# Attention with clusters, then experts: later turns for the second expert, own gathers first, one more drain

## The chip, the cores and the metric

The kernel runs on one core of one Trainium2 chip. The metric is the device time of one execution in microseconds. The kernel before took 926.72 us (median of three runs, 924.52 to 931.46).

## The reference, cut to what matters

The inputs are q, k and v of 4 batches, 8 heads, 768 positions and 64 dimensions, 16 centroids per head, two gates and the weights of 8 experts. A query sees the keys of its own cluster alone. The result, read as 3072 rows of 512, goes row by row through the one expert that its gate picks:

```python
for e in range(E):                      # E = 8, F = 1024
    mask = e_idx == e
    h = np.maximum(x[mask] @ w1[e], 0.0)
    ye = h @ w2[e]
    out[mask] = gate_w[mask, None] * eom[mask, e, None] * ye
```

The gate picks 400, 354, 531, 257, 408, 444, 274 and 404 rows for experts 0 to 7. How many rows an expert has decides which code runs for it.

## The kernel before, in words

The first 560 us are attention and routing: TensorE makes maxima, scores and values, and at the end every row of x stands in DRAM (`x_d`), with a list per expert of the numbers of its rows (`list_d`, read into `lst`). The rest is the expert stage, which the change is about.

**Sizes.** For every expert the program holds one branch for each of 41 sizes, 256 to 512 rows in steps of 8 and on to 768 in steps of 32. Each engine reads the size and jumps (`tc.Switch`). Up to 512 rows an expert is one chunk. Beyond that (`v >= NONE`, here expert 2 with 531 rows, run as 2 x 272) it is two chunks, and the second chunk's rows, 68 to each of four gathers, are the "own" gathers into `XG[2]` by the indices `lsxi`.

**One chunk.** `chunk` runs f = 0 to 7. In each step TensorE makes a hidden tile (`hidden`, L1145: 12 matmuls into `ps_h`), then projects the step before (`project`, L1164: 12 matmuls into `ps_y`), then does what `beside(f)` asks for. ScalarE and VectorE turn `ps_h` into `hh` and `hl` (L1152, L1153), and split a weight tile four steps ahead into `wh` and `wl` (L1043, L1044) from a staging buffer that SyncE loaded (L1038).

**Turns and gathers.** While expert e runs, GpSimd gathers the rows of expert e + 2 from `x_d` into `XG` (`gather`, L1047, four of 128 rows each), and the rows of expert e + 1, gathered earlier, are turned (`turn`: four transposes into `ps_xg`, L1133, a cast `xh`, L1134, a subtraction `xl`, L1135). In the kernel before, `after(f)` does one turn and one gather at each of f = 2 to 5 (`TF = 2`). For expert 1 the list itself is read only in expert 0 at f = 1 (`first_lists`), and its four gathers follow at once.

**Results.** Behind the chunk ScalarE and VectorE copy `ps_y` into `yt` (L1182). Four transposes per 128 rows, a scaling into `yo` and a scatter to the output (`finish`, L1209) follow: for most experts behind the next expert's chunk, for a large expert's first chunk within its second, for the last expert but one within the last, at f = 0 to 3 (`before`), and for the last one behind it. The program ends with the waits for all transfers, a drain of each engine and a barrier.

**What sets the order.** TensorE's, VectorE's and ScalarE's order within an expert is that of the code, or a scheduler's by priorities; GpSimd's within an expert is the scheduler's. Each engine runs its queue in order. GpSimd issues all gathers and scatters, on one queue.

Of the kernel before, what the change touches and what calls it, by code (L numbers as in the profile page):

```python
# [20 lines left out]
DM, E, FF = 512, 8, 1024  # L21
# [12 lines left out]
NVAR, NONE, XCH = len(SIZES), SIZES.index(512) + 1, 512  # L34
# [5 lines left out]
def tile_cluster_attention_moe(  # L40
# [10 lines left out]
    nc = tc.nc  # L51
# [114 lines left out]
    V, QD, KD, hold = {}, {}, {}, {}  # L166
# [764 lines left out]
    def maxs():  # L931
        for u in range(2, NU):
            yield from maxima(u)
            yield

    gx = maxs()
# [86 lines left out]
    XG, XH, XL = [None] * 3, [None] * 3, [None] * 3  # L1023
# [22 lines left out]
    def gather(xg, idx, t, n=P):  # L1046
        return nc.gpsimd.indirect_dma_start(  # L1047
            xg[0:n, t], None, x_d, bass.IndirectOffsetOnAxis(ap=idx[0:n, t:t + 1], axis=0),
            bounds_check=CAP - 1, oob_is_err=False,
        )  # L1050
# [54 lines left out]
    with tc.issue_after(hold['ctl'].ins), tc.issue_after(hold['act'].ins):  # L1105
# [8 lines left out]
        a, min_val=lo, max_val=hi, skip_runtime_bounds_check_because="counts of tokens bound it"  # L1114
# [6 lines left out]
    def w_ahead(e, f, own, nxt):  # L1121

        for n, fn in ((LL, w_load), (LS, w_split)):
            if f + n < NF:
                if own:
                    fn(e, f + n)
            elif nxt:
                fn(e + 1, f + n - NF)

    def turn(k, t):  # L1130
        ps = p_t.tile([P, NC, P], F32, name="ps_xg", tag="tr")
        for c in range(NC):
            nc.tensor.transpose(ps[:, c], XG[k][:, t, c * P:(c + 1) * P], ident)  # L1133
        nc.scalar.copy(XH[k][:, :, t], ps)  # L1134
        hold['xl', t] = nc.vector.tensor_tensor(XL[k][:, :, t], ps, XH[k][:, :, t].bitcast(F32), ALU.subtract)  # L1135
# [44 lines left out]
    def result(d, py, yt):  # L1180

        (nc.vector.tensor_copy, nc.scalar.copy)[d % 2](yt[:, d].rearrange("p t m -> p (t m)"), py[d])  # L1182

    def chunk(k, n4, py, beside, e=E):

        prev = None
        for f in range(NF):
            h = hidden(f, XH[k], XL[k], n4)
            if prev is not None:
                project(f - 1, prev, py, n4)  # L1190
            beside(f)
            prev = h
        hint(e)
        project(NF - 1, prev, py, n4)

    AE = {ET.Activation}
    TF = 2

    def finish(yt, ls, idx, t, others, eng=None, pool=None, tag="tr"):

        ps = (pool or p_t).tile([P, NC, P], F32, name="ps_yo", tag=tag)
        for d in range(NC):
            nc.tensor.transpose(ps[:, d], yt[:, d, t], ident)
        yo = mp.tile([P, DM], F32, name="yo", tag="yo", bufs=4)
        if eng is nc.vector:
            nc.vector.tensor_scalar(yo, ps.rearrange("p d c -> p (d c)"), ls[:, t, 1:2], None, ALU.mult)
        else:
            nc.scalar.activation(yo, ps.rearrange("p d c -> p (d c)"), AF.Copy, scale=ls[:, t, 1:2])  # L1208
        sc = nc.gpsimd.indirect_dma_start(  # L1209
            out, bass.IndirectOffsetOnAxis(ap=idx[:, t:t + 1], axis=0), yo, None,  # L1210
            bounds_check=CAP - 1, oob_is_err=False,
        )
        for o in others:
            tc.declare_no_dep(sc.ins, o.ins, reason="every token has a row of its own")
        others.append(sc)
# [3 lines left out]
    lsxi = mp.tile([P, 4], I32, name="lsxi")  # L1219

    def expert(e, v):
        n = SIZES[v]
        a, y = e % 2, YT[e % 2]
        others = []
        if e == 0:
            first_turn()

        def before(f):

            if e == E - 1 and f < 4:  # L1230
                finish(YT[1 - a], lst[:, e - 1], rowsi[:, e - 1], f, others)

        def after(f):
            if e + 1 < E and TF <= f < TF + 4:
                turn(1 - a, f - TF)
                if e + 2 < E:
                    gather(XG[a], rowsg[:, e + 2], f - TF)

        if v < NONE:
            def beside(f):  # L1240
                if e == 0 and f == 1:
                    first_lists()
                w_ahead(e, f, True, True)
                before(f)
                after(f)
            chunk(a, n // 4, PY, beside, e + 1)
            return

        n4 = n // 8
        nc.sync.dma_start(  # L1250
            lsx[0:n4], list_d[e * CAP + n // 2:e * CAP + n].rearrange("(p t) x -> p t x", t=4)
        )
        nc.vector.tensor_copy(lsxi[0:n4], lsx[0:n4, :, 0])
        for t in range(4):
            gather(XG[2], lsxi, t, n4)

        def beside1(f):
            if e == 0 and f == 1:
                first_lists()
            w_ahead(e, f, True, False)  # L1260
            before(f)
            if f >= 4:
                turn(2, f - 4)

        def beside2(f):
            w_ahead(e, f, False, True)
            if f < 4:
                finish(y, lst[:, e], rowsi[:, e], f, others)
            after(f)

        chunk(a, n4, PY, beside1)
        for d in range(NC):
            result(d, PY, y)
        chunk(2, n4, PY, beside2, e + 1)

        nc.vector.memset(rowsi[:, e], int(FAR))
        nc.vector.tensor_copy(rowsi[0:n4, e], lsxi[0:n4])
        nc.vector.tensor_copy(lst[0:n4, e], lsx[0:n4])
# [27 lines left out]
    rowsg = mp.tile([P, E, 4], I32, name="rowsg")  # L1306
    behind = mp.tile([1, 2], F32, name="behind")

    def first_turn():

        for t in range(4):
            turn(0, t)
            keep_warm(W3 if t < 3 else W4, ps=PY[t])
            if t % 2:
                with tc.issue_after(hold['xl', t].ins):
                    for f in ((1,), (2, 3))[t // 2]:
                        w_split(0, f)

        bh = nc.sync.dma_start(behind, XG[0][0:1, 3, 0:2])
        with tc.issue_after(bh.ins):  # L1320
            for f in range(NSTG, LL):
                w_load(0, f)

    def first_lists():
        sh = [P, E, 4]
        nc.gpsimd.dma_start(
            lst, list_d[0:E * CAP].rearrange("(e s) x -> e s x", e=E)[:, 0:512].rearrange("e (p t) x -> p e t x", t=4)
        )
        nc.vector.tensor_tensor(
            rows, slot4.rearrange("p (o t) -> p o t", o=1).broadcast_to(sh),  # L1330
            ctl[:, 3].rearrange("p (e o) -> p e o", o=1).broadcast_to(sh), ALU.is_ge,
        )
        nc.vector.tensor_scalar(rows, rows, FAR, None, ALU.mult)

        with tc.issue_after(hold['hl'].ins):
            nc.vector.tensor_scalar(rowsg, lst[:, :, :, 0], CAP - 1.0, None, ALU.min)
        with tc.issue_after(hold['hl'].ins):
            nc.vector.tensor_tensor(rowsi, rows, lst[:, :, :, 0], ALU.add)
        for t in range(4):
            gather(XG[1], rowsg[:, 1], t)  # L1340
        nc.gpsimd.memset(XG[2], 0.0)

    for e in range(E):
        for v in tc.Switch(vvar[e], NVAR, hint=f"expert{e}"):
            with tc.manual_schedule(engines=AE):
                expert(e, v)
        with tc.manual_schedule(engines={ET.PE, ET.Activation, ET.DVE}):
            others = []
            a = e if e == E - 1 else e - 1
            for d in range(NC):  # L1350
                result(d, PY, YT[e % 2])
                if d % 2 and 0 < e < E - 1:
                    for t in (d - 1, d):
                        finish(
                            YT[a % 2], lst[:, a], rowsi[:, a], t, others, (nc.scalar, nc.vector)[t % 2],
                            (p_h, p_t)[d // 2], ("h", "tr")[d // 2],
                        )
            if e == 0:
                keep_warm(W5, p_t, "tr")
            if e == E - 1:  # L1360
                for t in range(4):
                    finish(YT[a % 2], lst[:, a], rowsi[:, a], t, others, (nc.scalar, nc.vector)[t % 2])
# [39 lines left out]
```

## Time and profile before

| what | us |
|---|---|
| median of three runs | 926.72 |
| the profiled execution | 928.52 |
| its span, first to last instruction | 926.8 |
| TensorE busy (matmul) | 830.4 |
| GpSimd busy | 433.7 |
| mean granted clock of TensorE | 0.952 |

The span is cut by the engines' own instructions; the profiled execution's time holds 1.7 us more than the span. A timeline row gives an instruction's start and length, and in brackets how long its engine had stood idle and what ended that. An engine that stands idle costs time only if the end of the program waits for it; in the expert stage that is TensorE, and behind the last matmul it is GpSimd's queue.

### The profile page before, as it was taken

How to read it: one execution, taken by the hardware profiler on the slowest of the kernel's cores; microseconds unless marked ns; L12 is line 12 of the kernel's file. 1: busy time of each engine (PE TensorE's matmuls, PEld its weight loads, DVE VectorE, ACT ScalarE, POOL GpSimd, SP SyncE). 2: the span in 40 equal slices, each digit the busy share in tenths (PEclk: the TensorE clock that was granted, in tenths of full speed). 3: DMA queues.
4: the chain of work that ended last, by engine and by line, in shares of the span. 5: the costliest groups of instructions: out<-in, count | busy, mean ns of one | idle time of the engine just before them, and what ended most of it. 6: DMA issues, size and time to landing. Idle time of an engine off the chain costs nothing.

```text
span 926.8 us, 14485 instructions
## 1 busy us (share of the span) xinstructions
PE 830.4 (90%) x4907; PEld 633.4 (68%) x4907; DVE 501.7 (54%) x1013; ACT 394.1 (43%) x757; POOL 433.7 (47%) x329
## 2 busy tenths in 40 slices
PE   4798969999799998999989989799799799999991
PEld 3445646666566565666656446799799799999991
DVE  5767536567466576556764375445424455446511
ACT  3234445555255553555425543334325344335421
POOL 6634547767677766777575444500501321402201
PEclk9789879999999999999999999899989899999996
DMA  8652864565656555455110055743702644535301
GB/s 233 143 120 59 199 164 128 145 164 133 105 150 162 126 155 121 121 155 128 28 35 35 1 152 128 231 142 113 240 12 70 204 157 157 172 106 181 124 18 40
DMA packets 47387, 117.18 MB, mean 126 GB/s; under 512 B 11460, under 2 KB 13740, under 8 KB 47180
## 3 DMA queue, kind: packets, MB, share of 16 engines
q1 hardware_dynamic: 40300, 99.71, 40.1%
q0 software_dynamic: 6880, 15.28, 5.0%
q8 instruction: 60, 0.98, 0.5%
q14 instruction: 147, 1.20, 0.4%
HBM read 61.48 MB, written 15.95 MB: 84 GB/s over the span
## 4 chain that ended last, share of the span: by engine, by line
PE 43%; issue 21%; DMA 20%; DVE 10%; POOL 2%; SPq 1%; ACT 1%; POOLq 0%; DVEq 0%; ACTq 0%
PE ps_xt L487 14%; PE ps_ex L454 14%; DMA xg<-x_d,rowsg 7%; DMA out_dram<-yo,rowsi 6%; PE ps_mx L414 6%; DVE mx L418 5%; DMA x_d<-xn 3%; DMA xg<-x_d,rows 2%; PE ps_sm L508 2%; PE ps_as L217 2%; POOL out_dram L1209 1%; PE ps_xn L625 1%; DMA m<-qd 1%; PE ps_lg L578 1%; POOL xg L1047 1%
## 5 line engine op out<-in xcount | busy, mean ns | idle before, releaser
L418 DVE TENSOR_REDUCE mx<-ps_mx 128x1 f32<-128x384 f32 x360 | 181.9, 550 | 125.3 <-PE ps_mx L414 123.6
L459 ACT ACTIVATE ex<-ps_ex 128x384 f32<-128x384 f32 x384 | 169.7, 490 | 152.5 <-PE ps_ex L454 122.3
L474 POOL TENSOR_TENSOR es<-es,ex 128x768 f32<-128x768 f32 (+1 forms) x128 | 185.3, 1469 | 88.4 <-ACT ex L459 87.7
L454 PE MATMUL ps_ex<-m,s 128*128 128x384 f32 (+1 forms) x768 | 185.5, 362 | 7.1 <-DMA m<-nmt 7.0
L454 PEld LDWEIGHTS ps_ex<-m,s 128*128 128x128 f32 (+1 forms) x768 | 137.9, 197 | 45.8 <-issue 18.7
L487 PE MATMUL ps_xt<-ex,v 128*64 128x384 f32 (+1 forms) x768 | 148.0, 505 | 0.0
L1209 POOL DMA_INDIRECT out_dram<-yo,rowsi x36 | 37.0, 1027 | 230.0 <-ACT yo L1208 175.6
L414 PE MATMUL ps_mx<-s,m 96*128 96x384 f32 x360 | 110.8, 376 | 13.5 <-DVE xn L646 5.2
L487 PEld LDWEIGHTS ps_xt<-ex,v 128*64 128x64 f32 x768 | 52.4, 139 | 69.4 <-issue 66.2
L414 PEld LDWEIGHTS ps_mx<-s,m 96*128 96x128 f32 x360 | 68.8, 197 | 38.0 <-DVE mx L418 25.4
L1164 PE MATMUL ps_y<-hh,wh 128*128 128x272 f32 (+6 forms) x288 | 92.9, 323 | 0.0
L1044 DVE TENSOR_TENSOR wl<-wst,wh 128x1024 fp32r<-128x1024 f32 x64 | 78.3, 1225 | 26.4 <-ACT wh L1043 25.1
L1164 PE MATMUL ps_y<-hh,wl 128*128 128x272 f32 (+6 forms) x288 | 92.4, 321 | 0.0
L1164 PE MATMUL ps_y<-hl,wh 128*128 128x272 f32 (+6 forms) x288 | 91.9, 322 | 0.0
L1153 DVE SCALAR_TENSOR_TENSOR hl<-ps_h,hh 128x272 fp32r<-128x272 f32 (+6 forms) x72 | 37.3, 517 | 100.8 <-ACT hh L1152 95.0
L1152 ACT ACTIVATE hh<-ps_h 128x272 fp32r<-128x272 f32 (+6 forms) x72 | 33.1, 459 | 123.9 <-PE ps_h L1145 110.3
L1145 PE MATMUL ps_h<-xh,wh 128*128 128x272 f32 (+6 forms) x288 | 63.8, 345 | 8.8 <-issue 7.0
L474 POOL TENSOR_TENSOR es<-ex,ex 128x768 f32<-128x768 f32 (+1 forms) x32 | 54.9, 1730 | 32.9 <-ACT ex L459 32.9
L1043 ACT CAST wh<-wst 128x1024 fp32r<-128x1024 f32 x64 | 66.6, 1043 | 3.8 <-DMA wst<-in_ww_dram 3.8
L1145 PE MATMUL ps_h<-xh,wl 128*128 128x272 f32 (+6 forms) x288 | 59.5, 329 | 0.0
L1145 PE MATMUL ps_h<-xl,wh 128*128 128x272 f32 (+6 forms) x288 | 59.3, 329 | 0.0
L1164 PEld LDWEIGHTS ps_y<-hh,wh 128*128 128x128 f32 x288 | 54.5, 189 | 0.5
(246 smaller groups left out, 1122.5 us busy)
## 6 DMA issues: line engine op xcount, KB each, us to landing
wst<-in_ww_dram SPq DMA_DIRECT2D x64, 512.0 KB
m<-hi SPq DMA_DIRECT2D x64, 192.0 KB
s<-hi SPq DMA_DIRECT2D x64, 192.0 KB
qd<-in_qT_dram SPq DMA_DIRECT2D x16, 384.0 KB
kd<-in_kT_dram SPq DMA_DIRECT2D x16, 384.0 KB
v<-in_vp_dram SPq DMA_DIRECT2D x16, 384.0 KB
m<-qd SPq DMA_DIRECT2D x32, 192.0 KB
s<-kd SPq DMA_DIRECT2D x32, 192.0 KB
```

The source lines that it names most:

```text
L414: nc.tensor.matmul(ps[:, :HF], m1[0:96, h, t * P:(t + 1) * P], s1[0:96, h, f * HF:(f + 1) * HF], start=True, stop=True,)
L418: nc.vector.tensor_reduce(mx2[:, h, t, f:f + 1], ps[:, :HF], AX.X, ALU.max)
L454: nc.tensor.matmul(ps[f][:, :HF], s[0:kk, h, kt * P:(kt + 1) * P], m[0:kk, h, f * HF:(f + 1) * HF], start=j == 0, stop=j == 1,)
L459: nc.scalar.activation(ex[:, cols(f)[0]], ps[f][:, :HF], AF.Exp, scale=0.125)
L474: eng.tensor_tensor(es, a, ex[:, o2], ALU.add)
L487: nc.tensor.matmul(xt[f][h * D:(h + 1) * D, :c.stop - c.start], V[u][:, kt, h * D:(h + 1) * D], ex[h][:, c], start=kt == 0, stop=kt == KT - 1,
L1043: nc.scalar.copy(wh, st)
L1044: nc.vector.tensor_tensor(wl, st, wh.bitcast(F32), ALU.subtract)
L1145: hold['mm'] = nc.tensor.matmul(psv, w[:, c * P:(c + 1) * P], x[:, c, :, 0:n4], start=k == 0, stop=k == 3 * NC - 1,)
L1153: hold['hl'] = nc.vector.scalar_tensor_tensor(hl[:, :n], ps[:, :n], 0.0, hh[:, :n].bitcast(F32), ALU.max, ALU.subtract)
L1164: nc.tensor.matmul(py[d].rearrange("p (t m) -> p t m", t=4)[:, :, 0:n4], w[:, DM + d * P:DM + (d + 1) * P], x, start=f == 0 and k == 0, st ...
L1209: sc = nc.gpsimd.indirect_dma_start(out, bass.IndirectOffsetOnAxis(ap=idx[:, t:t + 1], axis=0), yo, None, bounds_check=CAP - 1, oob_is_err ...
```

## The change

It does three things. In expert 0 the turns of expert 1 (and the gathers of expert 2 that stand with them) are placed at f = 4 to 7; for the other experts nothing moves. In an expert with more than 512 rows the gathers for the next expert but one are ordered behind the last of its own four gathers. In the last expert GpSimd gets one drain, ordered behind the fourth scatter of its loop.

```diff
--- before.py
+++ after.py
@@ -1231,10 +1231,15 @@
                 finish(YT[1 - a], lst[:, e - 1], rowsi[:, e - 1], f, others)
 
         def after(f):
-            if e + 1 < E and TF <= f < TF + 4:
-                turn(1 - a, f - TF)
+            if e == E - 1 and f == 5:
+                with tc.issue_after(others[3].ins):
+                    nc.gpsimd.drain()
+            first = TF if e else 4
+            if e + 1 < E and first <= f < first + 4:
+                turn(1 - a, f - first)
                 if e + 2 < E:
-                    gather(XG[a], rowsg[:, e + 2], f - TF)
+                    with tc.issue_after(hold['gx'].ins) if v >= NONE else nullcontext():
+                        gather(XG[a], rowsg[:, e + 2], f - first)
 
         if v < NONE:
             def beside(f):
@@ -1252,7 +1257,7 @@
         )
         nc.vector.tensor_copy(lsxi[0:n4], lsx[0:n4, :, 0])
         for t in range(4):
-            gather(XG[2], lsxi, t, n4)
+            hold['gx'] = gather(XG[2], lsxi, t, n4)
 
         def beside1(f):
             if e == 0 and f == 1:
```

VectorE at the end of expert 0, in the branch for 400 rows, before (`wl` is half of a split weight tile, `xl` half of a turn, `hl` half of a hidden tile):

```order
L1153 SCALAR_TENSOR_TENSOR hl<-ps_h,hh 128x400
L1044 TENSOR_TENSOR wl_5736<-wst_5724,wh_5728 128x1024
L1135 TENSOR_TENSOR xl_6055<-ps_xg,xh_6054 128x4x128
L1153 SCALAR_TENSOR_TENSOR hl<-ps_h,hh 128x400
L1044 TENSOR_TENSOR wl_5737<-wst_5725,wh_5729 128x1024
L1153 SCALAR_TENSOR_TENSOR hl<-ps_h,hh 128x400
L1178 SWITCH_STRIDE
L1178 ISA
L1178 BRANCH_PREFETCH_HINT
L1044 TENSOR_TENSOR wl_5738<-wst_5726,wh_5730 128x1024
L1398 UNCONDITIONAL_BRANCH
```

And now:

```order
L1044 TENSOR_TENSOR wl_5736<-wst_5724,wh_5728 128x1024
L1135 TENSOR_TENSOR xl_6055<-ps_xg,xh_6054 128x4x128
L1153 SCALAR_TENSOR_TENSOR hl<-ps_h,hh 128x400
L1044 TENSOR_TENSOR wl_5737<-wst_5725,wh_5729 128x1024
L1135 TENSOR_TENSOR xl_6055<-ps_xg,xh_6054 128x4x128
L1153 SCALAR_TENSOR_TENSOR hl<-ps_h,hh 128x400
L1178 SWITCH_STRIDE
L1178 ISA
L1178 BRANCH_PREFETCH_HINT
L1044 TENSOR_TENSOR wl_5738<-wst_5726,wh_5730 128x1024
L1135 TENSOR_TENSOR xl_6055<-ps_xg,xh_6054 128x4x128
L1403 UNCONDITIONAL_BRANCH
```

The last two turns stand in the last two steps, and the last `xl` is VectorE's last instruction before the branch. TensorE's transposes and ScalarE's casts moved with them.

GpSimd in expert 2's branch for 544 rows, before (`xg_6056` is `XG[2]`, `xg_5718` is `XG[0]`, for expert 4):

```order
L1398 UNCONDITIONAL_BRANCH
L1344 BRANCH_PREFETCH_HINT
L1047 DMA xg_5718<-x_d,rowsg 128x512 x4
L1047 DMA xg_6056<-x_d,lsxi 68x512 x4
L1209 DMA out_dram<-yo,rowsi 3072x512 x4
L1398 UNCONDITIONAL_BRANCH
```

And now:

```order
L1403 UNCONDITIONAL_BRANCH
L1349 BRANCH_PREFETCH_HINT
L1047 DMA xg_6056<-x_d,lsxi 68x512 x4
L1047 DMA xg_5718<-x_d,rowsg 128x512 x4
L1209 DMA out_dram<-yo,rowsi 3072x512 x4
L1403 UNCONDITIONAL_BRANCH
```

The two groups of four gathers have changed places. The drain stands in none of these rows; in the last expert's branch it is the instruction right behind the fourth scatter.

## Rows read from the trace of the kernel before

**Rows 1.** The page's busy times (busy us, share of the span, instructions) and the clock that TensorE was granted in 40 equal slices of the span, in tenths.

```profile
PE 830.4 (90%) x4907; PEld 633.4 (68%) x4907; DVE 501.7 (54%) x1013; ACT 394.1 (43%) x757; POOL 433.7 (47%) x329
PEclk9789879999999999999999999899989899999996
```

**Rows 2.** The waits of TensorE from 560 to 727 us: who waited <- what ended the wait: us in total, times, longest. The three longest.

```profile
PE ps_xg L1133 <- DMA xg<-x_d,lsxi: 7.2, 1, 7.2
PE ps_h L1145 <- issue: 6.7, 1, 6.7
PE ps_xg L1133 <- DMA xg<-x_d,rowsg: 4.7, 1, 4.7
```

**Rows 3.** Windows of the expert stage: from:to, us, then busy time (and instructions) of PE, PEld, DVE, ACT and POOL, then the granted clock, the share of the transfer engines and GB/s.

```profile
569.70:582.40 12.70, 12.70 (x69) 11.78 (x69) 7.06 (x11) 6.82 (x9) 3.15 (x3) 1.00 0.86 204
582.54:587.19 4.65, 0.00 (x1) 0.00 (x1) 2.06 (x3) 0.00 (x0) 3.73 (x4) 0.86 0.66 204
587.19:592.70 5.51, 5.51 (x18) 5.48 (x19) 0.69 (x1) 0.94 (x2) 4.29 (x5) 0.50 0.90 305
666.56:673.73 7.17, 0.01 (x2) 0.04 (x1) 0.44 (x1) 0.00 (x0) 2.88 (x3) 0.82 0.74 205
673.73:678.03 4.30, 4.30 (x20) 4.30 (x21) 0.72 (x2) 0.98 (x2) 0.00 (x0) 0.50 0.02 4
912.20:926.80 14.60, 0.00 (x0) 0.00 (x0) 0.00 (x0) 0.00 (x0) 0.01 (x1) 0.50 0.05 18
```

**Rows 4.** Timeline of TensorE: start us, us, engine, line, operation, tiles, shape [idle before <- what ended it]. The first turn of the first expert, two turns of expert 1 (within expert 0), and the first hidden matmuls and the first use of `hl` of expert 1.

```profile
565.32 0.63 PE L1133 MATMUL ps_xg<-ident,xg 128*128 128x128 f32 x4 [1.73 <-DMA xg<-x_d,rows]
587.19 1.12 PE L1133 MATMUL ps_xg<-ident,xg 128*128 128x128 f32 x4 [4.65 <-DMA xg<-x_d,rowsg]
604.33 0.60 PE L1133 MATMUL ps_xg<-ident,xg 128*128 128x128 f32 x4
617.12 1.01 PE L1145 MATMUL ps_h<-xh,wh 128*128 128x360 f32 x4
621.97 0.50 PE L1164 MATMUL ps_y<-hl,wh 128*128 128x360 f32 x2
```

**Rows 5.** Timeline of VectorE at the end of expert 0, with the same columns: the last turn's `xl`, the last `wl`, the copies of the result, and the first `hl` of expert 1.

```profile
605.58 0.69 DVE L1135 TENSOR_TENSOR xl<-ps_xg,xh 128x512 fp32r<-128x512 f32 x1 [0.56 <-ACT xh L1134]
613.05 1.23 DVE L1044 TENSOR_TENSOR wl<-wst,wh 128x1024 fp32r<-128x1024 f32 x1 [0.36 <-ACT wh L1043]
617.44 1.29 DVE L1182 COPY yt<-ps_y 128x512 f32<-128x512 f32 x2 [3.16 <-issue]
620.28 0.53 DVE L1153 SCALAR_TENSOR_TENSOR hl<-ps_h,hh 128x360 fp32r<-128x360 f32 x1 [1.55 <-ACT hh L1152]
```

**Rows 6.** Timeline of GpSimd: the issue of the first gather for expert 0 and of the first for expert 1.

```profile
560.15 1.63 POOL L1047 DMA_INDIRECT xg<-x_d,rows  x1 [7.05 <-DVE ctli L1099]
582.02 1.90 POOL L1047 DMA_INDIRECT xg<-x_d,rowsg  x1 [4.53 <-DVE rowsi L1338]
```

**Rows 7.** Timeline of GpSimd and TensorE at the start of expert 2: the last of the four scatters behind expert 1, the first gather for expert 4, the first own gather, and the first two turns of the own rows.

```profile
656.51 1.68 POOL L1209 DMA_INDIRECT out_dram<-yo,rowsi  x1 [0.30 <-issue]
658.95 1.04 POOL L1047 DMA_INDIRECT xg<-x_d,rowsg  x1 [0.76 <-issue]
664.25 1.45 POOL L1047 DMA_INDIRECT xg<-x_d,lsxi  x1 [0.30 <-issue]
673.73 1.09 PE L1133 MATMUL ps_xg<-ident,xg 128*128 128x128 f32 x4 [7.17 <-DMA xg<-x_d,lsxi]
679.17 0.60 PE L1133 MATMUL ps_xg<-ident,xg 128*128 128x128 f32 x4
```

**Rows 8.** Timeline of GpSimd in the last expert: the fourth scatter in its loop and the next instruction.

```profile
886.31 0.97 POOL L1209 DMA_INDIRECT out_dram<-yo,rowsi  x1 [3.95 <-ACT yo L1208]
907.41 0.97 POOL L1209 DMA_INDIRECT out_dram<-yo,rowsi  x1 [20.12 <-ACT yo L1208]
```

**Rows 9.** The queue instructions by line (engine and operation, count: shortest/median/longest ns, first to last start in us): INC_SWDGE_SEM from 565 to 590 us, the same from 860 to 890 us, the one at the end, the drains at the end, and TensorE's branches.

```profile
L1398 POOLq INC_SWDGE_SEM  x8: 441/476/509, 567.5 to 587.1; - x8
L1398 POOLq INC_SWDGE_SEM  x4: 1187/1202/1222, 873.9 to 881.2; - x4
L1363 POOLq INC_SWDGE_SEM  x1: 2096/2096/2096, 915.4 to 915.4; - x1
L1398 POOLq DRAIN  x3: 46/109/8134, 917.8 to 926.5; - x3
L1398 PEldq COMPARE_BRANCH  x16: 321/570/6287, 561.1 to 902.3; - x16
```

**Rows 10.** The transfers that GpSimd issued, by tiles, with their counts, from the view of the DMA issues.

```profile
out_dram<-yo,rowsi POOLq DMA_INDIRECT x36
xg<-x_d,rowsg POOLq DMA_INDIRECT x28
list_d<-lists,rposi POOLq DMA_INDIRECT x24
xg<-x_d,rows POOLq DMA_INDIRECT x4
xg<-x_d,lsxi POOLq DMA_INDIRECT x4
lst<-list_d POOLq DMA_DIRECT2D x1, 32.0 KB
```

## The prediction

> **What bounds the kernel now.** I read the busy times and the clock line first, then TensorE's waits over the expert stage, then the windows around each wait, the timelines of the engines that end them, and last GpSimd's own queue behind the last scatter. TensorE is busy 90% of the span [rows 1], so the time goes where it stands still, and a stop can be paid twice: once idle, once more at the lower clock afterwards. In the expert stage (from about 560 us) three stops are over 4 us [rows 2]: 4.7 us for a gather with `rowsg`, 7.2 us for a gather with `lsxi`, and 6.7 us before a `ps_h` that no named work ends. The first two are what two parts of the change touch; the third lies at a branch and is left alone. [...] The idle of 1.73 us before the very first expert's rows [rows 4] left the clock at 1.00 [rows 3].
>
> After the last work the span still lasts 14.6 us in which no engine computes [rows 3]. Of it, GpSimd's queue holds one INC_SWDGE_SEM of 2.10 us and one DRAIN of 8.13 us [rows 9].
>
> **Part 1, the turns of expert 1.** The change adds no instruction: four turns (four transposes, a cast, a subtraction each) move from f = 2 to 5 to f = 4 to 7. In the trace the first is reached at 582.54 and its rows come at 587.19, since the gather was issued at 582.02 [rows 4, 6]. In the new order TensorE goes on with the hidden tile of f = 3, and meets the first turn two tiles later; a step without a turn takes (604.33 - 587.19 less the slow stretch's loss of 2.75) / 3 turns, 4.8 us with its turn, so some 4.4 us without, and it comes at about 582.5 + 2 x 4.4 = 591.3, 4 us behind the landing. The 4.65 us go. The half-speed stretch gives back half of 5.51, 2.75 us. The three later turns follow at 4.8 us each; the gathers behind the first are issued 1.3 us apart, so none is late.
>
> What the move costs stands at the other end. The last turn now lies in front of the last projection, and the last instruction of VectorE before the branch becomes `xl` in place of `wl`. A turn's `xl` starts 1.25 us after its transposes [rows 4, 5]: at 613.24 + 1.25 = 614.5 on the old scale, 1.44 us behind the `wl` at 613.05. Behind that instruction VectorE needed 4.4 us until its first copy, 3.16 of them with nothing to wait for that the profile shows, and its `hl` for expert 1 came at 620.28 [rows 5]; both slide by 1.44 us. TensorE first reads that `hl` at 621.97 [rows 4], and it would be ready at 620.28 + 1.44 + 0.53 = 622.25. I charge 0.3 us, with 0 and 1.5 as the ends. Expert 1 itself starts at 617.12 [rows 4], behind 614.5 + 0.7. The gathers for expert 3 that wait for these turns are late by a turn or two, but GpSimd has nothing else to issue before the scatters behind expert 1, so that is free. Weight loads issue on SyncE in the same order; one split moves forward with TensorE, and I cost it at nothing because its staging load was issued before the gathers. If that cover went, a split would hold `hh` and cost as much as the wait it replaces. **Part 1: 4.65 + 2.75 - 0.3 = 7.1 us, between 5.9 and 7.4.**
>
> **Part 2, the large expert's own gathers first.** Expert 2 alone takes this path. GpSimd issues four scatters until 658.2, then the four gathers of expert 4's rows (needed only an expert later), then the own ones from 664.25 on [rows 7]. TensorE stood at its turn from 666.56 and got its rows at 673.73, 9.48 us after that issue. Swapped, the first own gather is issued in the place of the other, 658.95. How long it takes there no row shows. Nearest from below: 5.17 us from issue to TensorE's start, twice, at 560.15 to 565.32 and 582.02 to 587.19 [rows 4, 6], with no transfer of GpSimd's close ahead. From above: the 9.48 us of the same gather with four transfers ahead. In the new place four scatters are ahead, of which the first three have had longer to land, so I take the middle, 7.3: rows at 666.3, just in time, with 664.1 and 668.4 as ends (no wait, or 1.9 us). The other three are issued 1.5 us apart and are needed 3.5 us apart. The four gathers now behind them have until expert 3. So 7.17 us of idle and half of 4.30 us of slow clock go, 9.3 in all. I take **9.0**, leaving 0.3 for a short wait; the lower end, 1.9 us waited and the clock falling all the same, is 9.3 - 1.9 - 2.1 = **5.3**.
>
> [...]
>
> **Part 3, the drain.** DRAIN stands three times at the end: 8134, 109 and 46 ns [rows 9]. The long one runs when all transfers have been waited for, and the next takes 0.1 us, so its length is work that one drain does away with. What work, the INC_SWDGE_SEM rows hint at: the same instruction takes 0.44 to 0.51 us around 580 us and 1.2 us around 880 us [rows 9]; it grows as GpSimd issues transfers. There are 36 + 28 + 24 + 4 + 4 + 1 = 97 of them [rows 10], and 8134 / 97 is 84 ns each. The added drain sits behind the fourth scatter of the last expert, which ends at 887.28, when 93 have been issued: some 7.8 us. GpSimd's next work starts at 907.41, after 20.1 us of idle [rows 8]; nobody waits for GpSimd in between, so it is free up to 20 us. At the end four transfers are left: 4 x 84 ns + 0.1 = 0.45 us in place of 8.13, and about 0.3 in place of 2.10 us. Both lie on the only path left there. **Gain 7.7 + 1.8 = 9.5**; ends 10.1 (both vanish) and 8.0 if the four scatters still in flight are kept, or nothing if the drain clears nothing.
>
> **The sum.** 7.1 + 9.0 + 9.5 = 25.6 us. The profiled execution took 928.5 us, 1.8 above the median of the three runs (926.7): 902.9 against the one, 901.1 against the other. I forecast **902**. With the ends (19.2 to 26.8) and the spread of the runs it is 898 to 912.
>
> **Rivals.**
> - *The final drain stays long* (0.12). If its price is fixed once transfers have been used, the added one hides its 8 us under the matmuls and the last still takes 8.1: 902 + 9.5 = 911.5. Against it: 109 and 46 ns right behind. For it: none of the traces has a drain between transfers. [...]
> - *One of the two waits returns* (0.10): the own gathers are slow by themselves, or weights hold ScalarE in expert 0. It costs 7 to 9 us: about 910. For it: the transfer engines were 0.66 to 0.90 busy there [rows 3].
> - *Two of the three gains fail* (0.03): about 919.
> - *Slower* (0.03). Place: TensorE's branch between experts. Its longest took 6.29 us against a median of 0.57 [rows 9], and is the 6.7 us stop that no work ends. Such a stop and half-speed afterwards, as behind 587.19, are 6.7 + 2.75 = 9.4 us. Moved code and earlier arrival could make more branches long; three more of the seven would cost 28 us and give 931, above the old time. Against it: one in sixteen is that long, and no code is added to TensorE's queue.
>
> The cases put 0.94 on faster by over 1% (below 917.5), 0.03 on no change and 0.03 on slower; 1% is about what a measurement of this kernel can tell, its three runs being 0.75% apart. Reaching to the first two rivals, the range is 897.5 to 912.5.
>
> **What would show it.** Part 1: no wait for `rowsg` before a transpose near 582 us, and a clock of 1.00 there; wrong if VectorE's `hl` holds the first `ps_y` of expert 1 for over 1.5 us. Part 2: the `lsxi` gather issued near 652 on the new scale and a wait under 2 us. Part 3: a DRAIN of 7 to 8 us some 20 us before the last scatter, a last long one under 1 us, and the time behind the last scatter down from 14.6 to about 5 us. A last drain of 8 us, or a stop of the old size at either gather, would make the forecast wrong.

## The result, and the profile after

The changed kernel takes **902.3 us** (median of four runs, 899.49 to 904.81), beside 929.1 us of the kernel before on the same chip: a ratio of 0.973, 95% interval 0.967 to 0.979. Every ratio below is a kernel's time over that of the kernel before, run beside it. The forecast was 902 (897.5 to 912.5). Its profiled execution took 902.92 us with a span of 901.1.

The page's lines that answer to [rows 1]:

```profile
PE 825.6 (92%) x4907; PEld 628.8 (70%) x4907; DVE 500.4 (56%) x1013; ACT 394.0 (44%) x757; POOL 435.1 (48%) x329
PEclk9889879999999999899999999999999999999898
```

TensorE's waits of the changed kernel from 560 to 720 us, all that the view lists, as in [rows 2]:

```profile
PE ps_xg L1133 <- DMA xg<-x_d,rows: 1.4, 1, 1.4
PE ps_h L1145 <- issue: 1.2, 1, 1.2
PE ps_y L1164 <- ACT hh L1152: 1.0, 1, 1.0
PE ps_h L1145 <- ACT yt L1182: 0.6, 1, 0.6
```

Both waits for gathers are gone, and the 6.7 us stop before a `ps_h` is too. To see where the time went, both traces are cut at the first hidden matmul of each expert and at the last matmul. First the kernel before, by windows with the columns of [rows 3]: experts 0, 1, 2, 3, 6 and 7, and what lies behind the last matmul.

```profile
570.97:617.12 46.15, 41.50 (x217) 39.88 (x216) 19.97 (x25) 16.84 (x24) 16.65 (x14) 0.93 0.70 204
617.12:652.68 35.56, 35.56 (x227) 35.41 (x225) 18.98 (x24) 15.22 (x23) 0.07 (x1) 1.00 0.35 115
652.68:725.36 72.68, 58.11 (x452) 57.48 (x450) 27.94 (x45) 25.21 (x44) 21.41 (x20) 0.93 0.37 119
725.36:755.37 30.01, 29.13 (x224) 28.91 (x225) 16.30 (x22) 14.24 (x23) 4.50 (x4) 0.94 0.47 145
...
837.86:867.60 29.74, 28.83 (x228) 28.62 (x226) 18.27 (x25) 15.08 (x25) 4.67 (x4) 1.00 0.43 141
867.60:908.35 40.75, 40.25 (x224) 38.94 (x224) 13.42 (x18) 13.68 (x22) 8.83 (x9) 1.00 0.18 65
908.35:926.80 18.45, 0.00 (x0) 0.00 (x0) 0.75 (x1) 0.22 (x1) 2.95 (x4) 0.55 0.14 50
```

The same windows of the changed kernel:

```profile
568.90:609.01 40.11, 38.91 (x217) 37.50 (x216) 19.94 (x25) 15.83 (x22) 16.89 (x15) 1.00 0.78 233
609.01:645.67 36.66, 35.70 (x224) 35.27 (x225) 18.86 (x24) 16.20 (x25) 0.06 (x1) 1.00 0.35 113
645.67:702.30 56.63, 55.97 (x451) 55.53 (x450) 25.81 (x42) 24.79 (x44) 18.67 (x17) 1.00 0.41 120
702.30:730.67 28.37, 27.48 (x224) 27.27 (x225) 18.14 (x25) 15.36 (x25) 9.57 (x9) 1.00 0.65 217
...
813.03:848.85 35.82, 29.05 (x228) 28.66 (x226) 20.07 (x27) 16.04 (x26) 8.57 (x8) 0.97 0.52 171
848.85:891.65 42.80, 42.30 (x224) 40.81 (x224) 11.60 (x15) 12.82 (x20) 5.10 (x5) 0.95 0.05 17
891.65:901.10 9.45, 0.00 (x0) 0.00 (x0) 0.75 (x1) 0.22 (x1) 2.95 (x4) 0.65 0.29 96
```

Read by differences: expert 0 is 6.0 us shorter, expert 1 is 1.1 longer, expert 2 is **16.1** shorter and not 9, expert 3 is 1.6 shorter, experts 6 and 7 are 6.1 and 2.1 **longer**, and the end is 9.0 shorter. The start of the first window has moved by 2.1 us, before any changed code; over all 14 traces read here it lies between 568.9 and 576.5 us. With 0.1 for experts 4 and 5 that is the 25.7 us between the spans. The gain in expert 2 and the loss in 6 and 7 are one thing, seen in TensorE's queue. First TensorE's branches in the changed kernel from 600 to 880 us (columns as in [rows 9]), then its stop at the longest:

```profile
L1403 PEldq COMPARE_BRANCH  x14: 402/526/6067, 603.1 to 842.5; - x14
```

```profile
848.85 1.36 PE L1145 MATMUL ps_h<-xh,wh 128*128 128x408 f32 x3 [6.30 <-issue]
```

The branch of 6.29 us behind expert 2 [rows 9] has become short, and one of 6.07 us stands behind expert 6. The stop of 6.7 us has moved, and so has the slow stretch behind it: the lower clock lies in expert 7 now (0.95) and no longer in expert 3 (0.94).

The queue of GpSimd at the end: the added drain, the last INC_SWDGE_SEM, and the drains behind the last transfer.

```profile
L1236 POOLq DRAIN  x1: 8888/8888/8888, 869.4 to 869.4; - x1
L1368 POOLq INC_SWDGE_SEM  x1: 249/249/249, 899.3 to 899.3; - x1
L1403 POOLq DRAIN  x3: 46/109/377, 899.5 to 900.8; - x3
```

The timeline of GpSimd around the added drain, the fourth scatter and the next:

```profile
869.62 0.97 POOL L1209 DMA_INDIRECT out_dram<-yo,rowsi  x1 [3.95 <-ACT yo L1208]
890.71 0.97 POOL L1209 DMA_INDIRECT out_dram<-yo,rowsi  x1 [20.12 <-ACT yo L1208]
```

The drain's record begins at 869.4, ahead of the scatter that it has to follow; 869.4 + 8.89 is 878.3, which is 7.7 us behind that scatter's end at 870.6. GpSimd still has 12 us before its next work.

### The profile page after: what moved, and what is told of

Its sections match the earlier page's. It is cut to its first block, busy times and chain, and to the rows that moved or that the text cites. A ratio compares the mean times of both kernels' runs of the same rounds, so it can differ in the third digit from the quotient of the medians.

```text
span 901.1 us, 14495 instructions
## 1 busy us (share of the span) xinstructions
PE 825.6 (92%) x4907; PEld 628.8 (70%) x4907; DVE 500.4 (56%) x1013; ACT 394.0 (44%) x757; POOL 435.1 (48%) x329
## 4 chain that ended last, share of the span: by engine, by line
PE 54%; DMA 20%; issue 13%; DVE 9%; POOL 1%; SPq 1%; ACT 1%; POOLq 0%; DVEq 0%; ACTq 0%
PE ps_xt L487 15%; PE ps_ex L454 14%; DMA out_dram<-yo,rowsi 8%; PE ps_mx L414 6%; DMA xg<-x_d,rowsg 5%; DVE mx L418 5%; PE ps_y L1164 4%; PE ps_h L1145 4%; DMA x_d<-xn 3%; PE ps_sm L508 2%; PE ps_as L217 1%; PE ps_xn L625 1%; POOL out_dram L1209 1%; DVE xn L646 1%; DMA m<-qd 1%
```

## The experiments

**The three parts, each alone.** Each is the kernel before with one part of the diff; cut lines are marked by three dots.

```diff
+            first = TF if e else 4
+            if e + 1 < E and first <= f < first + 4:
+                turn(1 - a, f - first)
...
+                    gather(XG[a], rowsg[:, e + 2], f - first)
```

> Only the turns of expert 1 are moved. My theory: no wait for rowsg near 588 us and a granted clock of 1.00 there, which gives 4.65 + 2.75 us; at the end of expert 0 up to 2 us are given back, for the trace of the changed kernel shows two stops of about 1 us there, at the branch and before the first ps_y of expert 1. Net 5 to 7 us, a ratio of 0.992 to 0.995. The lsxi wait of 7.2 us, the last DRAIN of 8.1 us and the last INC_SWDGE_SEM of 2.1 us stay as they were. Rival (the gain belongs to the three parts together): the rowsg stop goes but the lsxi stop grows by as much, for TensorE comes earlier to a transfer that comes no earlier; ratio 0.998 to 1.002.

Measured: ratio **0.994** (0.991 to 0.997), 5.4 us. Expert 0 and expert 1 in its trace as windows, and from TensorE's timeline the stop that stays in expert 2:

```profile
571.33:610.76 39.43, 39.00 (x217) 37.57 (x216) 20.50 (x27) 15.68 (x22) 16.65 (x14) 1.00 0.81 243
610.76:646.46 35.70, 35.69 (x224) 35.27 (x225) 18.97 (x24) 16.21 (x25) 0.06 (x1) 1.00 0.34 109
```

```profile
668.02 1.09 PE L1133 MATMUL ps_xg<-ident,xg 128*128 128x128 f32 x4 [7.37 <-DMA xg<-x_d,lsxi]
```

Expert 0 is 6.7 us shorter and expert 1 only 0.1 longer: here the moved turns cost nothing at the branch, and the up to 2 us that the expectation gave back there did not come. The `lsxi` stop did not grow by what was gained (7.37 after 7.17), so the rival falls.

```diff
+                    with tc.issue_after(hold['gx'].ins) if v >= NONE else nullcontext():
...
-            gather(XG[2], lsxi, t, n4)
+            hold['gx'] = gather(XG[2], lsxi, t, n4)
```

> Only the large expert's own gathers are put first. My theory: no wait for lsxi over 2 us, first own gather landing 6 to 7.5 us after its issue, clock 1.00 behind it; 9.0 us less, a ratio of 0.990. The rowsg wait of 4.7 us in expert 0 and the drain of 8.1 us stay. Rival (the own gathers are slow by themselves, 9.5 us from issue to use whatever is ahead): a wait of about 4 us is left, the clock falls all the same, and the gain is 3 us, a ratio of 0.997.

Measured: ratio **0.990** (0.986 to 0.993), 9.7 us. Its `lsxi` wait is 0.4 us. The `rowsg` wait of expert 0 stands, and the long branch is behind expert 6 although this part alone was made, as TensorE's timeline shows:

```profile
590.21 1.11 PE L1133 MATMUL ps_xg<-ident,xg 128*128 128x128 f32 x4 [5.59 <-DMA xg<-x_d,rowsg]
...
859.46 1.02 PE L1145 MATMUL ps_h<-xh,wh 128*128 128x408 f32 x2 [5.09 <-issue]
```

```diff
+            if e == E - 1 and f == 5:
+                with tc.issue_after(others[3].ins):
+                    nc.gpsimd.drain()
```

> Only the drain is added. My theory (84 ns for each transfer issued since the last drain): added drain of 7.8 to 8.9 us behind the fourth scatter, last long DRAIN 0.4 to 0.5 us, last INC_SWDGE_SEM about 0.3 us, 14.6 us behind the last work become about 5; 9.5 us less, a ratio of 0.990. Both waits for gathers stay as they were. Rival (in the changed kernel the end is short because the gathers run in another order or earlier): DRAIN 8 us at the end as before, ratio 1.000.

Measured: ratio **0.989** (0.985 to 0.993), 10.3 us. Its last long DRAIN is 378 ns and its INC_SWDGE_SEM 249 ns, with both gather waits in place (4.4 and 7.3 us). The end is short because of the drain. The three ratios multiply to 0.973, that of the whole change.

**One step earlier.** In the changed kernel:

```diff
-            first = TF if e else 4
+            first = TF if e else 3
```

> The changed kernel with the turns of expert 1 at f = 3 to 6 instead of 4 to 7. My theory (two costs against each other): the first turn is reached one step of 4.4 us earlier, at about 584.5 us, and its rows land at 587 us, so a wait of 2 to 3 us comes back, perhaps with a stretch at half speed behind it; the two stops of 1.2 and 1.0 us at the end of expert 0 go, since VectorE's last instruction before the branch is wl again. Net 0 to 2 us slower than the changed kernel: ratio to before 0.973 to 0.976. Rival (the stops at the end of expert 0 come from TensorE's long branch there, not from the last xl): they stay, and it is 2.5 to 4 us slower than the changed kernel, ratio 0.976 to 0.978.

Measured: ratio 0.975 (0.971 to 0.979). The first turn started at 587.38 without a wait, as its rows had landed at 587.0. What told was elsewhere in TensorE's timeline:

```profile
612.32 0.90 PE L1145 MATMUL ps_h<-xh,wh 128*128 128x360 f32 x4 [1.61 <-issue]
...
665.14 0.63 PE L1133 MATMUL ps_xg<-ident,xg 128*128 128x128 f32 x4 [3.19 <-DMA xg<-x_d,lsxi]
```

The stop at the end of expert 0 stays, at 1.6 us, with `wl` as VectorE's last instruction again. So it is not the last `xl` that makes it but TensorE's branch, here 4.3 us long. The other traces agree: a stop of 1.1 to 1.9 us stands there in the five whose branch at that place took 3.7 to 4.6 us, and none of 0.9 us or more in the nine where it took 2.0 to 3.4 us, some of them with the last `xl` behind `wl` too. And the first own gather landed only 10.7 us after its issue, which brought 3.2 us of waiting back in expert 2. The wait forecast at the first turn was wrong, the rival's point on the branch right.

**What a drain costs.** The drain moved into expert 3, behind its fourth gather:

```diff
-            if e == E - 1 and f == 5:
-                with tc.issue_after(others[3].ins):
-                    nc.gpsimd.drain()
...
-                        gather(XG[a], rowsg[:, e + 2], f - first)
+                        g = gather(XG[a], rowsg[:, e + 2], f - first)
+                    if e == 3 and f == 5:
+                        with tc.issue_after(g.ins):
+                            nc.gpsimd.drain()
```

> The changed kernel with its drain moved from the last expert to expert 3, behind the fourth gather there; 69 transfers are issued before it, 28 after. My theory (84 to 96 ns for each transfer since the last drain): the drain in expert 3 takes 5.8 to 6.6 us under cover, the last DRAIN 2.35 to 2.8 us, the last INC_SWDGE_SEM between 0.25 and 2.1 us; 2 to 3.5 us slower than the changed kernel. Rival A (the first drain in a program clears something that does not grow again): last DRAIN 0.4 us and INC_SWDGE_SEM 0.25 us, the time that of the changed kernel. Rival B (a fixed price whenever many transfers were issued): last DRAIN 8 us, ratio to before 0.981 to 0.984.

Measured, by the queue instructions of GpSimd:

```profile
L1242 POOLq DRAIN  x1: 7627/7627/7627, 719.6 to 719.6; - x1
L1368 POOLq INC_SWDGE_SEM  x1: 792/792/792, 903.0 to 903.0; - x1
L1403 POOLq DRAIN  x3: 46/109/2675, 903.8 to 907.0; - x3
```

The expectation miscounted: the view of the DMA issues, from 722 us to the end, has 32 transfers of GpSimd behind the moved drain and not 28, so 65 stand before it and not 69.

```profile
out_dram<-yo,rowsi POOLq DMA_INDIRECT x24, 4.0
xg<-x_d,rowsg POOLq DMA_INDIRECT x8, 5.0
```

The last DRAIN is 2.68 us for these 32, 84 ns each, as it was for the 97 of the kernel before, and the stretch behind the last matmul is 11.4 us in place of 9.5. Both rivals fall. The drain in expert 3 is 7.63 us in its record; from the end of the gather ahead of it (720.95) it is 6.2 us, 96 ns for each of 65. The ratio, 0.977 (0.972 to 0.981), lies 2 us above that of the changed kernel run beside it, 0.974 (0.969 to 0.980); the intervals overlap, so it is the trace that shows the cost and not the time.

**The long branch.** The changed kernel once more, and then with idle code (`keep_warm(n)` stands for n weight loads of TensorE with their matmuls):

```diff
         if e == 0:
             first_turn()
+            if v == 0:
+                keep_warm(32, ps=PY[0])
```

> The changed kernel once more, beside which the next three are read. What is to be seen is which of its stops belong to the program and which to one execution. My theory: TensorE's long branch stands again between experts 6 and 7 (a stop of 5 to 6.5 us), for it did so in all three kernels with the own gathers first, and between experts 2 and 3 in all three without; the first own gather lands 5 to 11 us after its issue (6.1, 5.1 and 10.7 us so far), so the wait for lsxi lies between 0 and 3.5 us. Ratio to before 0.970 to 0.976. Rival: the long branch falls at random, and stands elsewhere this time.

> The changed kernel with 64 instructions of TensorE (32 weight loads with their matmuls) more in expert 0's branch for 256 rows, which is not taken: nothing that runs is added, but all of TensorE's code behind it lies 64 instructions later. My theory (the long branch comes from where the code between two experts lies in the pieces in which it is loaded; the own gathers first lengthened TensorE's code by two waits in each branch of experts 3 to 6, and so moved the stop from behind expert 2 to behind expert 6): the stop of 6 us between experts 6 and 7 goes or stands at another place. If it goes, with the slow clock behind it, 7 to 8.5 us less than the changed kernel: ratio to before 0.962 to 0.966. If it stands elsewhere, the ratio is that of the changed kernel. Rival (it comes from the timing of transfers and engines around expert 6): it stays between experts 6 and 7 with 5 to 6.5 us, ratio 0.970 to 0.976.

With 64 in place of 32:

> As the run before, with 128 instructions more in the branch that is not taken. My theory: again no stop of 5 us between experts 6 and 7; without one anywhere 7 to 8.5 us less than the changed kernel, ratio to before 0.962 to 0.966, with one elsewhere 0.970 to 0.976. Rival (timing): the stop between experts 6 and 7 stays.

Measured: the changed kernel 0.974 (0.969 to 0.980), with 64 idle instructions **0.964** (0.960 to 0.968), with 128 **0.963** (0.958 to 0.967). The first hidden matmul of expert 7 in the three, in that order:

```profile
849.06 1.36 PE L1145 MATMUL ps_h<-xh,wh 128*128 128x408 f32 x3 [6.47 <-issue]
```

```profile
847.11 0.99 PE L1145 MATMUL ps_h<-xh,wh 128*128 128x408 f32 x4 [0.31 <-PE ps_yo L1203]
```

```profile
848.81 0.43 PE L1145 MATMUL ps_h<-xh,wh 128*128 128x408 f32 x1 [0.43 <-PE ps_yo L1203]
```

The stop belongs to the program: it returned in the repeat. Instructions that are never executed remove it, so it is the place of TensorE's code, and not the traffic, that decides whether it stands there; what the traffic adds to its length is not separated.

The trace of the changed kernel shows what stands ahead of the branch's end. The branch runs from 842.51 to 848.57 us. On the transfer queue that the profile names `q8 instruction` no packet begins from 842.51 to 846.0, and from 846.0 to 848.57 one does, of 16 KiB (packets, MB, share of 16 engines):

```profile
q8 instruction: 1, 0.02, 2.4%
```

It ends at 847.09, 1.5 us before the branch does. In all eight traces with the long branch behind expert 2 or expert 6 such a packet begins 2.2 to 4.4 us after the branch does and ends 1.3 to 1.5 us before it; in the four kernels with idle code that have part 2 (two of them follow below) none begins within the branch behind expert 6. So the long branch ends behind such a packet in all eight. That it waits there for code to be loaded is my reading of the queue's name and of what the idle code did; no run shows it by itself.

In the run with 128, experts 6 and 7 take 29.26 and 40.75 us, 8.6 less than in the changed kernel. The same was tried on the kernel before, with 56 and 72 in `keep_warm`.

> The kernel before with 112 instructions of TensorE (56 weight loads with their matmuls) more in expert 0's branch for 256 rows, which is not taken. My theory (the long branch lies where a piece of TensorE's code ends among the 16 transposes between two experts; in the kernel before that is behind the 13th transpose after expert 2, and with a piece of 256 instructions a shift of 112 puts such an end among the transposes of no expert): the 6.7 us stop behind expert 2 goes, none over 3 us comes at another branch; 7 to 9 us less than before, ratio 0.990 to 0.993, and expert 2's stop at its own rows (7.2 us) stays. Rival (timing: the stop comes from expert 2's late rows and the transfers around it): it stays behind expert 2, ratio 1.00.

> As the run before, with 144 instructions. My theory: a shift of 144 puts the end of a piece behind the 9th of the transposes after expert 4, so the long stop (5 to 7 us, half-speed behind it) stands between experts 4 and 5 and no longer between 2 and 3; the time is that of the kernel before, ratio 0.997 to 1.003. Rival A (any shift frees the kernel of the stop): no stop over 3 us, ratio 0.990 to 0.993. Rival B (timing): it stays behind expert 2.

Measured: 0.987 (0.981 to 0.992) and 0.990 (0.987 to 0.994). The first hidden matmul of expert 3, and in the second kernel also that of expert 5:

```profile
715.45 0.75 PE L1145 MATMUL ps_h<-xh,wh 128*128 128x264 f32 x4 [0.72 <-ACT yt L1182]
```

```profile
723.11 0.75 PE L1145 MATMUL ps_h<-xh,wh 128*128 128x264 f32 x4 [0.92 <-ACT yt L1182]
...
791.90 1.06 PE L1145 MATMUL ps_h<-xh,wh 128*128 128x448 f32 x4 [0.33 <-PE ps_yo L1203]
```

There is no long stop between experts in either; expert 2's stop at its own rows stays in both (5.3 and 7.4 us). The first ratio is below the 0.990 to 0.993 expected, with an interval that reaches it. That the code's place decides is shown; my rule for the place, by which the second would have its stop behind expert 4, is refuted. The piece of 256 instructions in that rule is near what the trace of the kernel before shows: from 28.05 to 558.69 us, where TensorE has no branch, 22 packets of `q8 instruction` begin, and TensorE runs 5592 instructions, 254 for each packet. It stays open by what rule a place is bad.

**The own gathers.** Two runs on the changed kernel with the 128 idle instructions. In one the gathers are 128 rows long (the added rows are not used):

```diff
-        nc.vector.tensor_copy(lsxi[0:n4], lsx[0:n4, :, 0])
+        nc.vector.tensor_copy(lsxi, lsx[:, :, 0])
...
-            hold['gx'] = gather(XG[2], lsxi, t, n4)
+            hold['gx'] = gather(XG[2], lsxi, t)
```

> The changed kernel with the 128 idle instructions, and with its own gathers of the large expert made 128 rows long instead of 68; the 60 more rows are copies of one row and are not used. In the runs so far with these gathers first, the first one landed 5.1 to 10.7 us after its issue (median 6.8), the second 7.7 to 11.0 (median 9.2). Theory A (bytes and the traffic beside it decide): 60 more rows in each of four gathers are 0.49 MB more at some 200 GB/s, 2.4 us; the second to fourth land later by 1 to 3 us, and a wait of 0 to 3 us appears at the turns. [...] Ratio to before 0.961 to 0.967 either way.

The own gathers from issue to landing, first in the kernel with 128 idle instructions and 68 rows, then in this one. The times are those of the second and the third of the four in each:

```profile
DMA to landing us min/median/max: 6.8/7.8/8.9
```

```profile
DMA to landing us min/median/max: 5.4/5.7/6.1
```

More bytes land sooner in this one execution: the second and third with 128 rows needed less than the same two in any of the seven profiles with 68 (6.8 to 11.0), which speaks against theory A. The first did not gain: 5.8 us, within the 5.1 to 10.7 of 68 rows. GpSimd's queue (`q0`) kept a larger share of the 16 engines busy with the longer gathers, first from 662.5 to 663.5 us with 68 rows, while one gather was under way, then from 661.5 to 663 with 128, while two were:

```profile
q0 software_dynamic: 60, 0.08, 25.6%
```

```profile
q0 software_dynamic: 84, 0.28, 77.8%
```

A quarter of 16 is four engines' worth for one gather of 68 rows; two of 128 rows kept over 12 busy, more than the eight of two such quarters. Why the longer ones spread over more engines was not shown. The ratio is 0.967 (0.963 to 0.972), not better than with 68 rows, for nothing waits there in either. In the other run two gathers of expert 4 go ahead again:

```diff
-                    with tc.issue_after(hold['gx'].ins) if v >= NONE else nullcontext():
+                    with tc.issue_after(hold['gx'].ins) if v >= NONE and f - first >= 2 else nullcontext():
```

> The changed kernel with the 128 idle instructions, and with two of expert 4's four gathers put back ahead of the large expert's own ones. My theory (each gather ahead costs its issue, 1.3 us, and up to 0.8 us of landing: four ahead gave a wait of 7.2 to 7.4 us, none ahead 0 to 0.4 us in six of seven profiles): a wait of 2.5 to 4.5 us at the own rows, part of a slow stretch behind it; 3 to 6 us slower than the same kernel with none ahead, ratio to before 0.966 to 0.970. Rival (the wait belongs to the 68-row gathers by themselves or to all four ahead together): no wait over 1 us, ratio 0.961 to 0.965.

Measured, by TensorE's timeline and the window of expert 2:

```profile
667.79 0.92 PE L1133 MATMUL ps_xg<-ident,xg 128*128 128x128 f32 x4 [3.47 <-DMA xg<-x_d,lsxi]
```

```profile
650.42:712.37 61.95, 57.50 (x451) 57.10 (x449) 26.12 (x43) 24.47 (x44) 17.68 (x17) 0.97 0.36 107
```

The wait is 3.5 us, half of the 7.2 that four gathers ahead cost in the kernel before, and expert 2 takes 61.95 us in place of 56.60: a stop of 3.5 us costs 5.4, the rest by the lower clock behind it (0.53 from 667.79 to 671.40). The ratio, 0.971 (0.963 to 0.979), is just above the 0.966 to 0.970 expected, and its interval covers that of the same kernel with none ahead; the wait is shown by the trace, the loss of time by the window alone.

## Why the prediction was right

**Part 1: 7.1 us forecast, 4.9 measured in the whole change** (6.0 won in expert 0, 1.1 lost in expert 1), 6.6 alone. The main terms held. The first turn, its row landed before:

```profile
588.90 0.60 PE L1133 MATMUL ps_xg<-ident,xg 128*128 128x128 f32 x4
```

It starts without a wait, and the 5.51 us at a granted clock of 0.50 [rows 3] behind the old wait, half of which is the term of 2.75, are gone: the clock in expert 0 is 1.00 in place of 0.93. The term that was mis-sized is the 0.3 us for the end of expert 0 (bounds 0 and 1.5): there the changed kernel stops twice, 2.2 us together.

```profile
609.01 0.74 PE L1145 MATMUL ps_h<-xh,wh 128*128 128x360 f32 x3 [1.20 <-issue]
...
614.20 0.43 PE L1164 MATMUL ps_y<-hh,wh 128*128 128x360 f32 x1 [0.96 <-ACT hh L1152]
```

The cause was not the one named either. The first stop follows a branch of TensorE of 3.9 us (2.1 before, 3.1 in the run of part 1 alone, which has no such stop) and stays with `wl` last. The second, behind ScalarE's `hh` and below the 1.5 us that I had named as a sign of error, stands neither in that run nor in the repeat of the changed kernel.

**Part 2: 9.0 forecast, 9.6 measured**, as the sum over experts 2, 3, 6 and 7 (-16.1 - 1.6 + 6.1 + 2.1). The first own gather was issued at 652.10, forecast near 652; the ones for expert 4 follow behind all four:

```profile
652.10 2.22 POOL L1047 DMA_INDIRECT xg<-x_d,lsxi  x1 [0.95 <-PE ps_h L1145]
...
659.01 1.03 POOL L1047 DMA_INDIRECT xg<-x_d,rowsg  x1 [0.30 <-issue]
```

The turn at 659.40 did not wait. The landing forecast at 7.3 us was 6.1 there, and 5.1 to 10.7 in seven profiles with these gathers first: the middle was right, but one (turns at f = 3 to 6) lay beyond the upper bound of 9.48 and waited 3.2 us. The gain rests on a narrow margin: the rows landed 1.2 us before the turn in the changed kernel (658.2 to 659.4) and 0.1 to 2.2 us before it in the six profiles without a wait.

**Part 3: 9.5 forecast, 9.0 measured.** A last DRAIN of 0.38 us (0.45 forecast), an INC_SWDGE_SEM of 0.25 (0.3), an added drain of 7.7 us behind its scatter (7.8) under a cover of 20.1. That the price goes by transfers is shown by 32 of them costing 2.68 us, and 97 costing 8.13, the same 84 ns each. Rows and bytes do not set it: with 128 rows in place of 68 in the four own gathers the added drain's record is 8.89 us, as in the changed kernel. The rival of a fixed last drain fell.

**The rivals.** Neither of the two waits returned in the changed kernel. The slower one had its place right and its reason against wrong: I wrote that no code is added to TensorE's queue. Waits are, and the rows of the code that I read had not shown them. Those of TensorE at the turns from 570 to 905 us, before and after:

```profile
L1133 PEldq EVENT_SEMAPHORE  x23: 51/51/51, 596.2 to 854.2; - x23
```

```profile
L1133 PEldq EVENT_SEMAPHORE  x31: 51/51/51, 595.3 to 829.4; - x31
```

Eight more are executed. All kernels without idle code that have them have the long stop behind expert 6, and those without them have it behind expert 2, so these waits are the likely cause of the move, which brought no net gain; no run adds such waits alone. That the forecast of 902 was met to 0.3 us is in part luck: 2.2 us too much in part 1 stand against 2.1 us that the profiled execution was early at the first expert, which the change doesn't explain and which is small beside the 7.6 us by which that start varies over the traces.

## What to carry to other kernels

Before a queue's end is paid for, look whether it holds a drain whose length goes with the transfers issued (84 ns for each of 97 here), and put one where that engine is idle. Order transfers on one queue by when their rows are needed, and count a stop with the slow stretch behind it (3.5 us cost 5.4 here). Where a kernel branches, look for a branch of several us that no work ends (4.6 to 6.8 here): idle code in a branch not taken took it away and gave the fastest version here, 897 us (ratio 0.963). By what rule to choose its length is not known; four lengths were tried, two on each kernel, and all four took the stop away.

## What the runs showed of the hardware that was not expected

- A branch of TensorE took 0.3 to 6.8 us, and the stop before the next matmul up to 7.3, by where the code lies: 6.3 to 6.8 us behind expert 2 in three kernels without part 2, 4.6 to 6.2 behind expert 6 in five profiles with it, and none over 4 us between experts in six with idle code. Of the 238 branches of TensorE in the 14 traces, all 102 that took over 1 us ended 1.2 to 1.7 us after a 16 KiB packet of the queue `q8 instruction` had ended. What place of the code is bad no run here settles.
- DRAIN on GpSimd's queue takes 83 to 96 ns for each transfer issued since the last drain (97: 8.13 us; 93: 7.68 from the end of the scatter ahead; 65: 6.2 from the end of the gather ahead; 32: 2.68; 4: 0.38). The first drains of the other engines at the end of the kernel before take 0.01 to 0.02 us. The last INC_SWDGE_SEM grows likewise, 0.25 us after 4, 0.79 after 32 and 2.10 after 97.
- Own gathers of 68 rows (the second and third of the four) needed 6.8 to 8.9 us to land in one execution, the same with 128 rows 5.4 to 6.1 in another.
